# Attention and GELU MLP on one core: seven block products in place of eight in half of the first product of tiles 7 and 8

## The chip, the cores and the metric

The kernel runs on one core of one Trainium2 chip. The core has a matrix engine (TensorE, "PE" in the profile, its weight loads shown as "PEld"), a vector engine (VectorE, "DVE"), a scalar engine (ScalarE, "ACT"), GpSimd ("POOL") and SyncE ("SP"). Each engine takes its own instructions strictly in program order and waits on semaphores for the others; DMA queues move data. Matrix products land in PSUM, eight banks of 128 x 512 f32. The metric is device time in microseconds of one execution. The kernel before took 301.54 us, median of 13 runs from 298.81 to 305.87.

## The reference

A sliding-window attention (8 batches, 8 heads, 576 positions, head size 64, window 32 to each side) gives x, a matrix of 4608 tokens by 512; a two-layer MLP with a tanh-approximated GELU follows:

```python
scores = scale * np.matmul(q, k.transpose(0, 1, 3, 2))
scores = np.where(np.abs(pos[:, None] - pos[None, :]) <= window, scores, -1e9)
attn = softmax(scores); attn_out = np.matmul(attn, v)
x = attn_out.transpose(0, 2, 1, 3).reshape(B * S, H * D)     # 4608 x 512
h = x @ w_in                                                 # 512 -> 2048
g = gelu_tanh(h)
return g @ w_out                                             # 2048 -> 512
```

## The kernel before

The tokens are cut into nine tiles of 512 (t = 0 to 8). Each turn of the loop over t does the first product of tile t (x @ w_in and GELU, into gT), then its second product (g @ w_out), and in between the steps of the second product the attention of batch t+1, which makes the x of later tiles. All data are f16 on the way into PE and f32 in PSUM.

*First product.* `ffn_in(t, n)` computes one column, 128 of the 2048 hidden units for the tile's 512 tokens: four matmuls of 128x512 (L544) accumulate over the 512 model dimensions in one PSUM bank. There are sixteen columns, taken in the order n = 0 to 15, which `column` maps to n // 2 + 8 * (n % 2). `gelu` (L552, on ACT) reads the bank and writes that column of gT. The first three columns are begun at the end of the tile before, three quarters of each. Columns 1 and 2 use the two-bank buffer S0; the others go round the banks D, x1 and x0.

*Sums.* After every fourth column `sums` (L587, on DVE) makes four f16 sums of 128x512 from gT: S1 = A21 + A22, S2 = S1 - A11, S3 = A11 - A21, S4 = A12 - S2, where A11 to A22 are the blocks of g (two halves of the hidden units by two halves of the tokens).

*Second product.* `ffn_out(t, i)`, i = 0 to 111, is already in seven block products in place of eight (Winograd's form of Strassen's method); each is sixteen matmuls of 128x256 (L642). The seven pairs are in a list:

```python
WINO = [("A11", "B11", True), ("S2", "T2", True), ("A12", "B21", False), ("S3", "T3", False),
        ("S1", "T1", True), ("A22", "T4", False), ("S4", "B22", False)]
```

True means that the product starts a new accumulation in its bank; products 0, 2, 4 and 6 use bank x1 and products 1, 3 and 5 bank x0. After each product DVE copies or adds the bank into the f32 buffer y4 (M1 at L653, then L655, L657, L662, L665 or L668, L671, L680), and the next product in that bank may start only after that. So product 2 (A12 x B21) waits for the copy of M1. `store` sends the rows of y4 to DRAM from POOL's queue (L604, L606), in the last tile from SP's and ACT's.

*Order.* The order of every engine's instructions is the order of the program text; no scheduler moves them. Lists (`PLAN`, and for tile 7 `{5: "v-1", 31: "x-1"}`) say before which step i of the second product a piece of attention is placed. "v-1" in tile 7 is the last small group of attention: its matmuls (L462, L472) write banks D and O. Tile 8 has no attention in it. POOL issues the loads of v and the stores; SP issues the loads of q and k, which end with tile 5.

Of the kernel before, what the change touches and what calls it, by code (L numbers as in the profile page):

```python
# [36 lines left out]
def cut(b):  # L37
# [19 lines left out]
PLAN_1 = {12: "s0@0 s1@1 s2", 16: "m0 m1", 36: "m2", 45: "v0@1 v1 s-1@0", 52: "x0", 55: "x1", 62: "m-1",  # L57
          69: "s3@0 v2 v-1@1", 73: "m3", 81: "x2", 85: "x-1", 91: "v3 s4@1", 112: "x3 m4"}
PAIR_1 = {17: slice(0, 4), 40: slice(4, 8)}
# [5 lines left out]
RING = 1536  # L65
# [4 lines left out]
def kernel(  # L70
# [264 lines left out]
    def bank(i):  # L335

        return psM.tile([128, 512], FP32, name="mm", tag=f"x{i}")
# [183 lines left out]
    def column(t, n):  # L521

        return n // 2 + 8 * (n % 2) if t else n

    def ffn_in(t, n, d0=0, d1=4, then=True):
        fc = column(t, n)
        if t not in gTs:
            gTs[t] = gp.tile([128, NF, 512], FP16, name="gT", tag="gT")
        if d0 == 0:
            if t == 0:  # L530
                i = n % 8
                if i in (4, 6):
                    phs["S"] = psS.tile([128, 2, 512], FP32, name="ph2", tag=f"S{i // 2 - 2}")
                phs[fc] = psO.tile([128, 512], FP32, name="ph", tag="DO"[i]) if i < 2 else \
                    bank(i - 2) if i < 4 else phs["S"][:, i % 2, :]
            else:
                i = 3 if n in (1, 2) else 0 if n == 0 else (2, 1, 0)[n % 3]
                if n == 1:
                    phs["S"] = psS.tile([128, 2, 512], FP32, name="ph3", tag="S0")
                phs[fc] = bank(i) if i < 2 else phs["S"][:, n - 1, :] if i == 3 else \  # L540
                    psO.tile([128, 512], FP32, name="ph", tag="D")
        ph = phs[fc]
        for dc in range(d0, d1):
            nc.tensor.matmul(ph, w_in16[:, dc, fc * 128:fc * 128 + 128],  # L544
                             xT[:, dc, t * 512 % RING:t * 512 % RING + 512],
                             start=(dc == 0), stop=(dc == 3))
        if d1 == 4 and then:
            gelu(t, n)

    def gelu(t, n):  # L550
        fc = column(t, n)
        nc.scalar.activation(gTs[t][:, fc, :], phs[fc], AF.Gelu_apprx_tanh)  # L552
        if t and n % 4 == 3:
            sums(t, n // 4)

    wino = {}

# [18 lines left out]
        dst, x, y = wino["todo"][i]  # L576
        eng.tensor_tensor(dst, x, y, op=ALU.subtract)

    def sums(t, i):

        g, r = gTs[t], slice(2 * i, 2 * i + 2)
        A11, A21, A12, A22 = (g[:, r0 + 2 * i:r0 + 2 * i + 2, c:c + 256]
                              for r0 in (0, 8) for c in (0, 256))
        S1, S2, S3, S4 = (wino[f"S{n}"][:, r, :] for n in (1, 2, 3, 4))
        for dst, x, y, op in ((S1, A21, A22, ALU.add), (S2, S1, A11, ALU.subtract),
                              (S3, A11, A21, ALU.subtract), (S4, A12, S2, ALU.subtract)):
            nc.vector.tensor_tensor(dst, x, y, op=op)  # L587

    out_v = out.rearrange("(b p j) f -> b j p f", b=B, j=4)
# [226 lines left out]
    for t in range(NT):  # L816
        b = t + 1
        att = b < B
        if t:
            for fc in range(begun):  # L820
                ffn_in(t, fc, 3, 4, then=False)
            for fc in range(begun):
                gelu(t, fc)
            if att and b > 1:
                parts = cast_and_turn(b)
            for fc in range(begun, NF):
                ffn_in(t, fc)
                if t == 1 and fc == 3:
                    parts[0]()
                    combine(4, nc.vector)  # L830
                if t == 1 and 6 <= fc < 10:
                    cast_v(2, fc - 6)
                if t == 1 and 9 <= fc < 14:
                    parts[1](fc - 9)
                if t == 1 and fc == 8:
                    trans_tails(1, psO.tile([128, 8, 128], FP16, name="pt", tag="O"))
                if t == 2 and fc in (8, 9):
                    store(0, *later[1 if fc == 8 else 3])
                if t > 1 and fc == 8 and att:
                    pair_v(b, nc.vector.tensor_copy)  # L840
        plan = PLAN_0 if not t else PLAN_1 if t == 1 else PLAN if att else {5: "v-1", 31: "x-1"} if t == B - 1 else {}

        def group(g):
            return (b, g) if g >= 0 else (b - 1, 4)
# [6 lines left out]
        for i in range(113 if t else 65):  # L851
            if t and i == (4 if t > 1 else 46) and b + 1 < B:
                nc.gpsimd.tensor_copy(after, KLs[b % 2][:, 3, 0:1])
                load_v(b + 1)
            for act in plan.get(i, "").split():
                kind, at = act[0], int(act[act.index("@") + 1:]) if "@" in act else None
                g = int(act[1:].split("@")[0])
                if kind == "w":
                    if g == 3:
                        cast_w(wo[g], w_out16[:, 12:16, :], cs=(0, 1), on_dve=(0,))  # L860
                    else:
                        cast_w(wo[g % 3], w_out16[:, 4 * (g % 3):4 * (g % 3) + 4, :], on_act=(1, 3),
                               cs={1: range(4), 2: (0, 1), 5: (2, 3)}[g])
                elif kind == "e":
                    cast_vt(1) if g == 4 else cast_v(1, g)
                elif kind == "k":
                    cast_early(1, g, (nc.vector, nc.vector))
                    if g == 2:
                        cast_tails(0, nc.gpsimd, even)
                elif kind == "t":  # L870
                    trans_tails(0, spare(at)[0], even)
                elif kind == "r":
                    trans_pair(1, g, *spare(at), copy=nc.scalar.copy if g == 2 else nc.vector.tensor_copy)
                elif kind in "np":
                    pair = psS.tile([128, 2, 512], FP32, name="ps_od", tag=f"S{at}")
                    for x in range(2):
                        if kind == "n":
                            sum_up(1, g + x, pair[:, x, :], groups[(1, g + x)])
                        else:
                            ods[g + x] = (pair[:, x, :], lts[g + x])  # L880
                            times(1, g + x, pair[:, x, :], groups.pop((1, g + x)))
                    if kind == "n":
                        n = size(1, g)
                        lts[g], lts[g + 1] = lt4[:, g, :], lt4[:, g + 1, :]
                        for x in range(2):
                            nc.scalar.activation(lts[g + x][:, 0:n], pair[:, x, 0:n], AF.Ln)
                        for x in range(2):
                            nc.scalar.activation(lts[g + x][:, 0:n], lts[g + x][:, 0:n], AF.Exp, scale=-1.0)
                elif kind == "u":
                    cast_w(wo[g], w_out16[:, 12:16, :], on_act=(3,), cs=(2, 3))  # L890
                    cast_tails(1, nc.gpsimd)
                    load_qk(2)
                elif kind == "c":
                    if g == 1:
                        B12 = combine_w()
                    combine(g, nc.vector)
                elif kind == "s":
                    score(*group(g), at)
                    if t == 1 and g == 4:
                        load_table(gelu_set)  # L900
                elif kind == "d":
                    pair_chunk(b, g, nc.vector.tensor_copy)
                elif kind == "m":
                    mask(*group(g))
                elif kind == "v":
                    bb, gg = group(g)
                    o, d = weigh(bb, gg, at)
                    ods[g] = (o, invert(bb, gg, d))
                    if t and g < 0 and b + 1 < B:
                        load_vt(b + 1)  # L910
                    if t > 1 and g == (3 if att else -1):
                        load_table(gelu_set)
                else:
                    spread(*group(g), *ods[g])
            if t == 1 and i == 30:
                cast_vt(2)
                store(0, *later[0])
                store(0, *later[2])
            if t == 1 and i in PAIR_1:
                pair_v(2, nc.vector.tensor_copy, PAIR_1[i])  # L920
            if t == 0 and i < 64:
                ffn_out_0(*ORDER_0[i])
            elif t and i < 112:
                ffn_out(t, i)
# [36 lines left out]
```

## Time and profile before

| what | us |
|---|---|
| median of 13 runs | 301.54 |
| the profiled execution | 301.52 |
| its span, first to last instruction | 299.8 |
| tile 7: first L544 that completes a column, start | 244.33 |
| tile 7: third block product (product 2), start | 260.47 |
| tile 8: first L544 that completes a column, start | 271.14 |
| tile 8: third block product, start | 286.51 |
| end of the last matmul, about | 295.4 |

The profile is of one execution. A row of the timeline gives the start in us from the span's start, the length, the engine, the line of the kernel, the operation, what it writes and reads with partitions x elements, and in brackets how long the engine had been idle and whose result ended that. The starts of one engine's instructions can lie closer together than their lengths, because they overlap in its pipeline. The granted clock of PE was 1.00 in every stretch that holds matrix work.

### The profile page before, as it was taken

To read this page: it belongs to the slowest core of one execution; us is meant where nothing else is said; L and a number is where in the kernel's file an instruction comes from. 1 tells how busy PE (TensorE), PEld (TensorE's weight loads), DVE (VectorE), ACT (ScalarE), POOL (GpSimd) and SP (SyncE) were. 2 spreads that over 40 slices of the span, in tenths; PEclk is the share of its full clock that TensorE was granted. 3 is DMA by queue.
4 is the path that set the end of the run, shared out by engine and by line. 5 is a ranking of instruction groups with operands and counts; after the bars stand their busy time and mean duration, and the time that the engine had idled before them with its cause. 6 is when DMAs were issued, how large, how long until landed. Compare 5 with 4: busy or idle time off the path is not lost.

```text
span 299.8 us, 7125 instructions
## 1 busy us (share of the span) xinstructions
PE 286.8 (96%) x2893; PEld 179.6 (60%) x2893; DVE 195.0 (65%) x439; ACT 193.7 (65%) x307; POOL 90.7 (30%) x141
## 2 busy tenths in 40 slices
PE   7889899899999899999999999999999999999994
PEld 2534434446774488447854885478547864784583
DVE  4752577897976866957687769766876635442452
ACT  4866666679676776578567956695678666706600
POOL 3435415302654050605070606060700050015000
PEclk9999999999999999999999999999999999999999
DMA  7999998999899999898998996989792031004013
GB/s 221 266 300 384 357 277 231 246 202 204 213 207 192 239 238 159 143 121 210 180 204 145 225 168 148 148 201 178 113 186 33 3 100 43 2 3 137 2 35 105
DMA packets 116518, 50.73 MB, mean 169 GB/s; under 512 B 98007, under 2 KB 110039, under 8 KB 116486
## 3 DMA queue, kind: packets, MB, share of 16 engines
q1 hardware_dynamic: 87428, 37.88, 61.9%
q0 software_dynamic: 27936, 11.35, 25.5%
q10 hardware_dynamic: 1122, 1.06, 1.1%
q8 instruction: 22, 0.36, 0.5%
q14 instruction: 10, 0.08, 0.1%
HBM read 36.70 MB, written 9.44 MB: 154 GB/s over the span
## 4 chain that ended last, share of the span: by engine, by line
PE 64%; DMA 22%; SPq 7%; ACT 3%; DVE 1%; issue 1%; POOL 0%; DVEq 0%; ACTq 0%
PE mm L642 28%; PE mm L544 15%; PE ph L544 13%; DMA KT<-k 6%; DMA wst<-in_moe_w_in_dram 5%; DMA kr<-in_k_dram 4%; DMA tr<-in_q_dram 4%; PE ps_s L435 2%; PE ps_d L462 2%; DMA wst<-in_moe_w_out_dram 2%; SPq L173 2%; DMA tr<-in_k_dram 2%; PE ps_o L472 2%; SPq L227 2%; ACT gT L552 1%; SPq L149 1%
## 5 line engine op out<-in xcount | busy, mean ns | idle before, releaser
L544 PEld LDWEIGHTS <-w_in 128*128 128x128 f16 x576 | 55.9, 98 | 66.2 <-DVE w_in L215 0.6
L544 PE MATMUL mm<-xT,w_in 128*128 128x512 f16 x304 | 74.7, 379 | 0.0
L552 ACT ACTIVATE gT<-mm 128x512 f16<-128x512 f32 x76 | 45.1, 597 | 40.1 <-PE mm L544 39.4
L544 PE MATMUL ph<-xT,w_in 128*128 128x512 f16 x272 | 68.2, 379 | 0.3 <-POOL w_in L758 0.3
L606 POOL DMA_DIRECT2D out_dram<-y x55 | 32.2, 594 | 89.7 <-DVE y L671 75.6
L642 PEld LDWEIGHTS <-s 128*128 128x128 f16 x512 | 49.6, 98 | 6.0
L587 DVE TENSOR_TENSOR s<-gT 128x512 f16<-128x512 f16 x64 | 27.2, 425 | 33.2 <-ACT gT L552 33.2
L552 ACT ACTIVATE gT<-ph 128x512 f16<-128x512 f32 x68 | 37.9, 599 | 13.0 <-PE ph L544 13.0
L642 PE MATMUL mm<-t,s 128*128 128x256 f16 x376 | 44.7, 273 | 0.0
L642 PEld LDWEIGHTS <-gT 128*128 128x128 f16 x384 | 36.0, 98 | 6.6
L448 ACT ACTIVATE pe<-ps_s 128x960 f16<-128x960 f32 (+1 forms) x31 | 29.5, 975 | 14.2 <-PE ps_s L435 14.1
L642 PE MATMUL mm<-w_out,gT 128*128 128x256 f16 x256 | 32.8, 273 | 0.0
L95 ACT ACT_TABLE_LOAD x18 | 23.1, 1283 | 2.2 <-issue 1.9
L498 ACT ACTIVATE lt<-lt 128x480 f32<-128x480 f32 (+3 forms) x36 | 21.1, 585 | 1.1
L497 ACT ACTIVATE lt<-ps_d 128x480 f32<-128x480 f32 (+2 forms) x28 | 15.6, 555 | 9.3 <-PE ps_d L462 6.2
L457 DVE TENSOR_TENSOR pe<-pe,band 128x960 f16<-128x960 f16 x28 | 18.3, 668 | 1.2 <-ACT pe L448 1.2
L181 POOL DMA_DIRECT2D V<-in_v_dram x20 | 17.9, 913 | 1.1 <-issue 1.0
L472 PEld LDWEIGHTS <-V 128*64 128x64 f16 x520 | 14.0, 111 | 6.0 <-DVE V L191 1.4
L642 PE MATMUL mm<-t,gT 128*128 128x256 f16 x128 | 16.3, 273 | 0.0
L435 PE MATMUL ps_s<-QT,KT 64*64 64x128 f16 (+3 forms) x576 | 13.5, 216 | 2.3 <-DMA KT<-k 1.6
L435 PEld LDWEIGHTS <-KT 64*64 64x64 f16 x576 | 10.0, 106 | 8.4 <-issue 3.6
L642 PE MATMUL mm<-w_out,s 128*128 128x256 f16 x120 | 14.4, 273 | 0.0
(112 smaller groups left out, 324.3 us busy)
## 6 DMA issues: line engine op xcount, KB each, us to landing
kr<-in_k_dram SPq DMA_DIRECT2D x31, 256.0 KB, 11.5
qr<-in_q_dram SPq DMA_DIRECT2D x6, 1024.0 KB, 8.4
wst<-in_moe_w_in_dram SPq DMA_DIRECT2D x7, 512.0 KB, 8.4
V<-in_v_dram POOLq DMA_DIRECT2D x20, 128.0 KB, 8.8
wst<-in_moe_w_out_dram SPq DMA_DIRECT2D x2, 1024.0 KB, 12.0
wst<-in_moe_w_out_dram SPq DMA_DIRECT2D x4, 512.0 KB
qr<-in_q_dram SPq DMA_DIRECT2D x7, 256.0 KB, 6.8
out_dram<-y POOLq DMA_DIRECT2D x6, 192.0 KB, 5.7
```

The source lines that it names most:

```text
L95: nc.scalar.add_instruction(mybir.InstLoadActFuncSet(name=nc.get_next_instruction_name(), act_func_set_id=which, ins=[], outs=[]))
L181: nc.gpsimd.dma_start(V[:, c, :, :], v[b, :, 128 * c:128 * c + 128, :].rearrange("h p d -> p h d"))
L435: nc.tensor.matmul(sides[h][64 * half:64 * half + 64, 4 * n * r:4 * n * r + 4 * n].rearrange("k (j p) -> k j p", j=4)[:, :, p0 - q0:p1 - q ...
L448: nc.scalar.activation(pe, ps[:, :, 0:w], AF.Exp, scale=SCALE)
L457: nc.vector.tensor_tensor(pe, pe, m.rearrange("k (o j) p -> k o j p", o=1).broadcast_to(list(pe.shape)), op=ALU.mult)
L472: nc.tensor.matmul(o[64 * h:64 * h + 64, cols].rearrange("d (j p) -> d j p", j=4)[:, :, p0 - q0:p1 - q0], Vs[b % 2][:, slot, 2 * pr + h, : ...
L498: nc.scalar.activation(lt[:, 0:n], lt[:, 0:n], AF.Exp, scale=-1.0)
L544: nc.tensor.matmul(ph, w_in16[:, dc, fc * 128:fc * 128 + 128], xT[:, dc, t * 512 % RING:t * 512 % RING + 512], start=(dc == 0), stop=(dc = ...
L552: nc.scalar.activation(gTs[t][:, fc, :], phs[fc], AF.Gelu_apprx_tanh)
L587: nc.vector.tensor_tensor(dst, x, y, op=op)
L606: eng.dma_start(out_v[b, j, q0 + p:q0 + p + e, cols], yo[m:m + e, cols])
L642: nc.tensor.matmul(pys["apart"][:, 0:256] if apart else py[:, blk, :], lhsT, wino[w][:, f, :], start=(new and i % (8 if one else 16) == 0) ...
```

## The change

In tiles 7 and 8 the sixteen columns of the first product are split. Columns 0 to 3 and 12 to 15 stay as they were. The other eight are two units, A and B; each is a product of 2 x 2 blocks (two halves of 512 hidden units, from rows 2j and 8 + 2j of gT, by two halves of the 512 tokens, summed over two halves of the model dimensions) and is now made of the same seven block products as the second product, four matmuls of 128x256 each.

The sums of weights are made once: of unit B by POOL in tiles 3 and 4, of unit A by DVE and POOL in tile 6 (`in_w`). The differences of x are made by DVE, four ops of 128x512 f16, before tile 7's columns and in tile 7's second product for tile 8 (`in_x`). In a tile the products of each unit use three banks: "a" (products 0, 1, 3 and 5, bank O for A, x1 for B), "b" (product 2, a half of S1) and "c" (products 4 and 6, a half of S0). Three copies per unit take the running sum out of bank "a" into f32 buffers `sa` and `sb` (DVE, ACT, DVE), three additions on DVE put banks "b" and "c" onto them, and GELU reads three of the four blocks from these buffers and the fourth from bank "a". The order of all this is written out in the list MIX: a digit is a column, A0 a product, s0A a copy, cA00 an addition, g a GELU, t the first two and u the last two of the four sums of a group. Columns 3, 12 and 14 use bank D, columns 13 and 15 bank x0.

```diff
+MIX = ("3 g3 A0 s0A B0 s0B A2 B2 cA00 cB00 A1 s1A A4 B1 s1B gA00 gB00 B4 t0 u0 12 A3 s3A B3 s3B g12 cA11 cB11 13 "
+       "A5 B5 gA11 gB11 g13 14 gA10 gB10 A6 B6 cA01 cB01 g14 15 gA01 gB01 t1 t2 g15 t3 u1 u2 u3").split()
+UNITS = {"A": 1, "B": 2}
...
-                i = 3 if n in (1, 2) else 0 if n == 0 else (2, 1, 0)[n % 3]
+                i = 3 if n in (1, 2) else 0 if n == 0 else (2, 1, 0)[n % 3] if t < NT - 2 else (2, 0)[n % 2 if n > 3 else 0]
...
+    def in_w(eng, unit, *which):
...
+        for x in which:
+            dst, a, b, op = ((S1, A21, A22, ALU.add), (S2, S1, A11, ALU.subtract),
+                             (S3, A11, A21, ALU.subtract), (S4, A12, S2, ALU.subtract))[x - 1]
+            eng.tensor_tensor(dst, a, b, op=op)
+    def in_x(t):
...
+        xc = hp.tile([128, 4, 2, 256], FP16, name="xc", tag="q16" if t % 2 else "k16")
...
+        for dst, a, b in ((T1, B12, B11), (T2, B22, T1), (T3, B22, B12), (T4, B21, T2)):
+            nc.vector.tensor_tensor(dst, a, b, op=ALU.subtract)
+    def in_product(unit, n):
+        a, w, new = WINO[n]
+        if n == 0:
+            phs[unit, "a"] = psO.tile([128, 512], FP32, name="pu", tag="O") if unit == "A" else bank(1)
+        elif n in (2, 4):
+            which = "b" if n == 2 else "c"
+            if unit == "A":
+                phs[which] = psS.tile([128, 2, 512], FP32, name="pu2", tag="S1" if n == 2 else "S0")
+            phs[unit, which] = phs[which][:, "AB".index(unit), :]
+        ps = phs[unit, "b" if n == 2 else "c" if n in (4, 6) else "a"]
+        lhs, rhs = mixed[unit, "w"][a], mixed["x"][w]
+        for h in range(2):
+            for d in range(2):
+                nc.tensor.matmul(ps[:, 256 * h:256 * h + 256], lhs[:, d, 128 * h:128 * h + 128], rhs[:, d, :],
+                                 start=(n in (0, 2, 4) and h == d == 0), stop=(h == d == 1), skip_group_check=True)
+    def in_mixed(t):
+        if "A" not in mixed:
+            mixed["A"] = rawp.tile([128, 3, 512], FP32, name="sa", tag="qr")
+            mixed["B"] = rawp.tile([128, 3, 512], FP32, name="sb", tag="kr")
+        place = {"00": (0, "b"), "01": (1, "c"), "11": (2, "c")}
+        for step in MIX:
+            kind, rest = step[0], step[1:]
+            if kind in UNITS:
+                in_product(kind, int(rest))
+            elif kind == "s":
+                n, unit = int(rest[0]), rest[1]
+                (nc.scalar.copy if n == 1 else nc.vector.tensor_copy)(
+                    mixed[unit][:, (0, 1, None, 2)[n], :], phs[unit, "a"])
+            elif kind == "c":
+                x, which = place[rest[1:]]
+                x = mixed[rest[0]][:, x, :]
+                nc.vector.tensor_tensor(x, phs[rest[0], which], x, op=ALU.add)
+            elif kind == "g" and rest[0] in UNITS:
+                r, c, j = int(rest[1]), int(rest[2]), UNITS[rest[0]]
+                src = phs[rest[0], "a"] if rest[1:] == "10" else mixed[rest[0]][:, place[rest[1:]][0], :]
+                nc.scalar.activation(gTs[t][:, 8 * r + 2 * j:8 * r + 2 * j + 2, 256 * c:256 * c + 256],
+                                     src.rearrange("p (h c) -> p h c", h=2), AF.Gelu_apprx_tanh)
+            elif kind == "g":
+                fc = column(t, int(rest))
+                nc.scalar.activation(gTs[t][:, fc, :], phs[fc], AF.Gelu_apprx_tanh)
+            elif kind in "tu":
+                sums(t, int(rest), slice(0, 2) if kind == "t" else slice(2, 4))
+            else:
+                ffn_in(t, int(step), then=False)
...
-    def sums(t, i):
+    def sums(t, i, which=slice(0, 4)):
...
-                              (S3, A11, A21, ALU.subtract), (S4, A12, S2, ALU.subtract)):
+                              (S3, A11, A21, ALU.subtract), (S4, A12, S2, ALU.subtract))[which]:
...
-            for fc in range(begun, NF):
+            if t >= NT - 2:
+                if t == NT - 2:
+                    in_x(t)
+                in_mixed(t)
+            for fc in range(begun, NF if t < NT - 2 else 0):
...
+            if t == NT - 2 and i == 60:
+                in_x(t + 1)
+            if t in (3, 4) and i == 92:
+                in_w(nc.gpsimd, "B", *((1, 2) if t == 3 else (3, 4)))
+            if t == NT - 3 and i in (86, 90):
+                in_w(*((nc.vector, "A", 1, 2) if i == 86 else (nc.gpsimd, "A", 3, 4)))
```

More of the change, by code (lines that the diff above doesn't have):

```diff
@@ L554, in gelu @@
             sums(t, n // 4)
+    mixed = {}
+    def in_w(eng, unit, *which):
+        i = UNITS[unit]
+        A11, A12, A21, A22 = (w_in16[:, d:d + 2, c + 256 * i:c + 256 * i + 256] for c in (0, 1024) for d in (0, 2))
+        if (unit, "s") not in mixed:
+            halves = [(rawp if unit == "A" else yp).tile([128, 2, 2, 256], FP16, name="wc" + unit + str(x),
+                                                         tag=("qr", "kr")[x] if unit == "A" else "yo") for x in range(2)]
+            mixed[unit, "s"] = [half[:, x] for half in halves for x in range(2)]
+        S1, S2, S3, S4 = mixed[unit, "s"]
+        mixed[unit, "w"] = dict(A11=A11, A12=A12, A22=A22, S1=S1, S2=S2, S3=S3, S4=S4)
+        for x in which:
+            dst, a, b, op = ((S1, A21, A22, ALU.add), (S2, S1, A11, ALU.subtract),
+                             (S3, A11, A21, ALU.subtract), (S4, A12, S2, ALU.subtract))[x - 1]
+            eng.tensor_tensor(dst, a, b, op=op)
@@ new lines, in in_x @@
+    def in_x(t):
+        pos = t * 512 % RING
+        B11, B12, B21, B22 = (xT[:, d:d + 2, pos + c:pos + c + 256] for d in (0, 2) for c in (0, 256))
+        xc = hp.tile([128, 4, 2, 256], FP16, name="xc", tag="q16" if t % 2 else "k16")
+        T1, T2, T3, T4 = (xc[:, x] for x in range(4))
+        mixed["x"] = dict(B11=B11, B21=B21, B22=B22, T1=T1, T2=T2, T3=T3, T4=T4)
+        for dst, a, b in ((T1, B12, B11), (T2, B22, T1), (T3, B22, B12), (T4, B21, T2)):
+            nc.vector.tensor_tensor(dst, a, b, op=ALU.subtract)
```

## The prediction

> **What bounds the kernel now.** I read the page's busy shares first, then the chain that ended last, then the granted clock, and last the timeline of the two tiles that the change touches. The page's first and fourth parts:
>
> ```profile
> PE 286.8 (96%) x2893; PEld 179.6 (60%) x2893; DVE 195.0 (65%) x439; ACT 193.7 (65%) x307; POOL 90.7 (30%) x141
> ...
> PE 64%; DMA 22%; SPq 7%; ACT 3%; DVE 1%; issue 1%; POOL 0%; DVEq 0%; ACTq 0%
> ```
>
> TensorE (PE) is busy nearly always and carries most of the chain; DVE is a third idle on average. That average is no help: what counts is which engine is last inside tiles 7 and 8. Busy time by stretch (columns: length, then busy us and instructions of PE, PEld, DVE, ACT, POOL, then clock, DMA share, GB/s); the rows are tile 7's first product and second, tile 8's first and second, and the end:
>
> ```profile
> 242.28:255.99 13.71, 13.71 (x67) 6.25 (x64) 5.32 (x14) 8.67 (x16) 3.99 (x8) 1.00 0.27 77
> 255.99:269.09 13.10, 12.96 (x123) 11.35 (x122) 6.13 (x11) 4.33 (x6) 0.45 (x1) 1.00 0.00 1
> 269.09:282.80 13.71, 13.71 (x67) 6.25 (x64) 5.32 (x14) 8.49 (x15) 5.00 (x10) 1.00 0.27 78
> 282.80:296.30 13.50, 12.60 (x114) 10.96 (x112) 6.58 (x13) 0.74 (x2) 0.00 (x0) 1.00 0.17 52
> 296.30:299.80 3.50, 0.00 (x0) 0.00 (x0) 0.00 (x0) 0.00 (x0) 0.00 (x0) 0.80 0.39 99
> ```
>
> Both first products are gapless on PE, at full clock. Now the hand-over from first to second product of tile 8 (start, length, what; in brackets the idle time before):
>
> ```profile
> 282.15 1.03 PE L544 MATMUL ph<-xT,w_in 128*128 128x512 f16 x4
> ...
> 283.01 1.91 PE L642 MATMUL mm<-w_out,gT 128*128 128x256 f16 x16
> 283.21 0.60 ACT L552 ACTIVATE gT<-ph 128x512 f16<-128x512 f32 x1 [0.27 <-PE ph L544]
> 283.84 0.42 DVE L587 TENSOR_TENSOR s<-gT 128x512 f16<-128x512 f16 x1 [1.90 <-ACT gT L552]
> 284.30 0.42 DVE L587 TENSOR_TENSOR s<-s,gT 128x512 f16<-128x512 f16 x1
> 284.64 0.42 DVE L587 TENSOR_TENSOR s<-gT 128x512 f16<-128x512 f16 x1
> ...
> 284.76 1.91 PE L642 MATMUL mm<-t,s 128*128 128x256 f16 x16
> 284.98 0.42 DVE L587 TENSOR_TENSOR s<-gT,s 128x512 f16<-128x512 f16 x1
> 285.31 0.68 DVE L653 COPY y<-mm 128x512 f32<-128x512 f32 x1
> ...
> 286.51 1.91 PE L642 MATMUL mm<-w_out,gT 128*128 128x256 f16 x16
> ```
>
> After the last GELU only four sums stand on DVE ahead of the copy of M1 (L653). The third block product (286.51) accumulates into the bank that this copy reads, so it may not start before it; the copy ends at 285.99, 0.52 us early. That slack is the number to watch. Tile 7 shows one stall, in the chain: the D bank is not free for the group "v-1" until column 15's GELU is done.
>
> ```profile
> 255.50 0.88 PE ph L544 x4
> 256.40 0.61 ACT gT L552
> 257.05 0.35 PE ps_d L462 x2
> ```
>
> **The change, part by part.** All times below are us after a tile's first L544 matmul that completes a column (tile 8: 271.14; tile 7: 244.33).
>
> *Removed on PE.* Per tile, 32 matmuls of 512 become 56 of 256. Eight of 512 take 1.73 (chain), so 0.2157 each; sixteen of 256 take 286.51 - 284.76 = 1.75, so 0.109 each, their weight loads included. 32 x 0.2157 = 6.90 against 56 x 0.109 = 6.12: 0.78 saved per tile if nothing waits. The first product would end at 11.1 in place of 11.86.
>
> *Removed in tile 7.* Bank D is last used by column 14, not 15, so its stall (256.75 to 257.05) goes: 0.30. Next is the GELU of column 14, which I place at 11.64, before PE gets there (11.8).
>
> *Added on DVE per tile.* Four copies and six additions from PSUM, 128x512 f32. Rows L653 and L662 have 0.69; the next op may start 0.61 after (258.92 to 259.53 in tile 7). Bounds on the spacing 0.61 and 0.69; I take 0.61, which is measured. The sums keep their count of sixteen: 0.46 after an op whose result is needed (283.84 to 284.30), otherwise 0.34.
>
> *Added and moved on ACT.* Two copies (bounds 0.59 as L622's and 0.63 as L498's 512; 0.59 taken) and six of the sixteen GELUs now read f32 from SBUF. No row has such a GELU; a GELU from PSUM is spaced 0.49 (272.05 to the end of three, 1.57 later), and an exponential of 512 from SBUF (L498) lasts 0.63. Bounds 0.49 and 0.60, taken 0.52: the 0.03 by which L498's row exceeds L552's 0.60.
>
> *The new schedule*, in program order per engine, with PE results visible 0.42 (512) and 0.31 (256) after the last matmul's start as in the rows above, and 0.06 for a release of PE. PE: column 3 to 1.51, A0 1.95, B0 2.38, A2 2.82, B2 3.26, A1 3.69, A4 4.13, B1 4.57, B4 5.00, column 12 5.87, A3 6.30, B3 6.74, column 13 7.60, A5 8.04, B5 8.48, column 14 9.34, A6 9.78, B6 10.21, column 15 11.10. DVE: s0A 2.18, s0B 2.79, cA00 3.49 (it waits for B2 too), cB00 4.10, t0 and u0 4.71 to 6.27, then s3A not before A3 is visible: 6.53, s3B 7.14, cA11 7.75, cB11 8.36 to 9.05. So no bank makes PE wait, within 0.1, until here. ACT: gA11 8.44, gB11 9.05 (it waits for cB11), g13 9.57, gA10 10.06, gB10 10.55, g14 11.04, gA01 11.53 to 12.16, gB01 to 12.68, g15 12.57 to 13.17. In the kernel before, the last GELU ended at 283.81 - 271.14 = 12.67; so ACT is later though PE is earlier.
>
> *The added wait.* DVE's t1 (S1, S2 of unit A) waits for gA01, the ACT instruction before it, and all other sums but group 0's stand behind it: t1, t2, t3, u1, u2, u3, twelve ops. From 12.19: three pairs of 0.46 + 0.34 and six of 0.34 are 4.44, so the M1 copy starts at 16.63 and ends at 17.32. Behind DVE stands PE: block product n=0 starts at 11.21 (x1 is held by gB10), n=1 at 13.23 (x0 is held by g15), its rows 4 and 6 wait for t2 and t3 (0.36 and 0.58), and n=2 waits for M1 until 17.38, 1.46 of it idle. Before, n=2 started at 286.51 - 271.14 = 15.37: tile 8 loses 2.01. In tile 7 it started at 260.47 - 244.33 = 16.14; the group v-1 (0.46 on PE) now hides inside the wait, so n=2 again starts at 17.38: 1.24 lost. The 0.78 and the 0.30 are inside these differences. From n=2 on each eviction keeps its place, about 1 us of idle DVE before each, so nothing is won back.
>
> *The rest, at nothing, with its cover.* in_x of tile 7: four ops of 0.34 to 0.46 on DVE after 243.35, done at about 0.6, and s0A is at 2.18. in_x of tile 8, about 1.5, between C11 and U3 in tile 7: DVE has 1.05 free there and n=5 needs U3 only 1.75 after n=3; 0.5 late is covered, and without that cover it would cost 0.5. Two unit-A sums in tile 6 (0.8): DVE is idle 0.70 before 240.84; the copy after it may slip 0.1, and bank x0 is wanted only at 242.39. The six sums on POOL in tiles 3, 4 and 6 go ahead of the stores in its queue, which waits there for L671 (23.95 before 241.83); POOL casts of 512 last 0.6 to 0.87, so two delay stores by about 2 at most, if they run late, and nobody reads the stores but the next tile's evictions, a tile later. No DMA is added, SP's queue is untouched. The Trainium skill (SBUF — State Buffer, "Who interferes with whom") says that a DVE op with two SBUF inputs and a GpSimd op that reads SBUF lock each other out; no row here shows a GpSimd sum beside DVE. By that page each of the six could hold DVE up by one op, an estimate of 1 each, which the idle DVE of those spots would take.
>
> *Sum.* +2.01 + 1.24 = +3.25. The profiled execution took 301.52 (span 299.80 and 1.72 around it), next to the median of 301.54: 301.52 + 3.25 = **304.8**. With the unknowns at their cheap ends (spacing of PSUM reads 0.55, below any row, and no release time) n=2 starts at 17.0, which is +2.5; with all at their dear ends (ACT 0.60, DVE 0.70) at 17.86, which is +4.2. So 304.0 to 305.7.
>
> **Rivals.**
>
> *Faster (the other side): DVE's twelve sums are done when PE wants M1.* Then tile 8 reaches n=2 at 11.10 + 3.49 = 14.59 (-0.78), tile 7 at 15.05 (-1.09): 299.65. For it: DVE's share in tile 8's second product is only 6.58 of 13.50. Against it: 0.34 and 0.46 are measured, and the order on DVE is fixed. It decides when M1 is copied 1.63 earlier in each tile, that is when the 5.1 from gA01 to M1's end become 3.5.
>
> *About level: ACT reaches gA01 sooner.* cA01 ends at 11.13, and ACT gets there only at 11.53 with five GELUs queued since 9.05. If it kept up, t1 could start at 11.2, 1.0 earlier per tile: +1.2, 302.7. Against it: gB11 cannot precede cB11, which hangs on A3.
>
> *Slower still: PE's clock falls in the new gaps.* PE gets waits of 0.1, 0.3, 0.4, 0.6 and 1.5 in a row of 6 us. The clock row falls below 1.00 only in the last 3.5, where PE does nothing: 0.80. A loss of 0.2 over 3.5 is 0.7 per tile: +1.4, 306.2. The Trainium skill (TensorE: Matmul & The Clock Gate, "What's actually happening") puts the gate at an idle window of about 3.4, and no gap here is that long, so by it nothing is added; the same page ("A second HAM failure mode: psum-queue depth-cycling") warns that frequent short idling between bank groups makes the clock swing. By that the price would be half the work of one window, an estimate of 1.7 per tile and 308.2 in all; no row here shows it.
>
> *It does not do what it says:* the 256-column blocks run at the weight loads' pace. L642's rows exclude it: same shape, 0.109.
>
> **How the numbers follow.** Forecast 0.70, level 0.13 (0.09 of it within 0.5%, the rest just above), clock 0.08, faster 0.08, the rest 0.01. A measurement of this kernel tells about 0.5% (1.5 us) from no change; so faster 0.08, same 0.09, slower 0.83. The range takes in the forecast's 304.0 to 305.7, the level case and the clock's 306.2, and half a us of scatter of medians (single runs go from 298.81 to 305.87): 302.3 to 306.7. It leaves out the faster case.
>
> **What would show it.** Right: in tile 8 the first product ends about 0.75 sooner; the M1 copy is preceded on DVE by twelve sums without a gap; the third block product's wait, 1 to 2 us, is put down to that copy; n=2 begins near 17.4 in both tiles. Wrong: sums starting before gA01, an idle DVE before M1, or PE waiting inside the first product (then the PSUM reads are dearer than 0.61). A granted clock under 1.00 between 255 and 300 would be the clock rival.

## The result and the profile after

The changed kernel takes **307.39 us** (median of 11 runs, 304.55 to 313.40) against 301.94 for the kernel before (median of 48). The ratio is 1.018, with a 95% interval from 1.0142 to 1.0218: it is slower by 5.4 us (4.3 to 6.6). The forecast was 304.8, with 302.3 to 306.7 as its range: the direction was right, the size was outside. Ratios here and below are made from undisturbed executions of both kernels, so a ratio can differ from the quotient of two medians.

Line numbers of the kernel after: L553 matmuls of the columns, L605 the new block products, L625 additions, L561, L629 and L633 GELU, L670 sums of gT, L725 second product, L736 copy of M1, L738 and L740 the next evictions, L466 masks of attention, L471 the matmuls of attention's denominators, L580 sums of weights, L190 and L194 loads of v. From here on, "after" a tile's start means after its first L553 that completes a column (L544 in the kernel before); these starts are 247.14 and 275.17 for tiles 7 and 8.

First part of the page, busy time of each engine:

```profile
PE 287.3 (94%) x2941; PEld 183.9 (60%) x2941; DVE 215.0 (70%) x469; ACT 194.3 (64%) x311; POOL 97.0 (32%) x147
```

PE's busy time is nearly the same (286.8 before), while the span grew from 299.8 to 305.7. So the loss is waiting. Busy time by stretch (length, then PE, PEld, DVE, ACT, POOL, clock, DMA share, GB/s), here from each tile's start on: tile 7's first product and second, tile 8's first product and, to 302.20, its second:

```profile
247.14:258.05 10.91, 10.91 (x80) 7.63 (x79) 7.46 (x15) 7.19 (x14) 2.21 (x5) 1.00 0.30 89
258.05:275.17 17.12, 15.38 (x134) 12.01 (x132) 11.69 (x27) 5.86 (x9) 2.50 (x5) 1.00 0.06 16
275.17:286.40 11.23, 11.23 (x81) 7.72 (x80) 7.30 (x14) 7.51 (x15) 2.92 (x6) 1.00 0.26 72
286.40:302.20 15.80, 13.05 (x113) 10.69 (x111) 9.92 (x22) 1.96 (x4) 0.00 (x0) 1.00 0.16 46
```

Both first products are still without a gap, and the first matmul of the second product starts at 11.23 in both tiles (258.37 and 286.40). In the second products PE is idle for 1.74 and 2.75 (the latter about 0.8 of it behind the last matmul). The hand-over of tile 8, from the timeline:

```profile
286.70 0.65 ACT L629 ACTIVATE gT<-sa 128x512 f16<-128x512 f32 x1
287.22 0.65 ACT L629 ACTIVATE gT<-sb 128x512 f16<-128x512 f32 x1
287.38 0.43 DVE L670 TENSOR_TENSOR s<-gT 128x512 f16<-128x512 f16 x1 [0.51 <-ACT gT L629]
...
289.92 1.26 PE L725 MATMUL mm<-t,s 128*128 128x256 f16 x10 [0.40 <-DVE s L670]
...
291.45 0.42 DVE L670 TENSOR_TENSOR s<-gT,s 128x512 f16<-128x512 f16 x1
291.79 0.68 DVE L736 COPY y<-mm 128x512 f32<-128x512 f32 x1
292.53 1.69 PE L725 MATMUL mm<-w_out,gT 128*128 128x256 f16 x14 [1.34 <-DVE y L736]
```

GELU gA01 starts at 286.70 - 275.17 = 11.53, twelve sums follow on DVE without a gap, the copy of M1 starts at 16.62, and the third block product at 17.36. Tile 7 shows the same:

```profile
263.76 0.68 DVE L736 COPY y<-mm 128x512 f32<-128x512 f32 x1
...
264.50 1.69 PE L725 MATMUL mm<-w_out,gT 128*128 128x256 f16 x14 [1.34 <-DVE y L736]
```

The chain that ended last has the same two links in tile 8, three of the twelve sums and the copy:

```profile
290.87 1.01 DVE s L670 x3
291.87 0.61 DVE y L736
292.48 0.04 issue
292.53 4.53 PE mm L725 x40
```

The third block product starts, after the tile's start:

| | tile 7 | tile 8 |
|---|---|---|
| before | 16.14 | 15.37 |
| forecast for after | 17.38 | 17.38 |
| after | 17.36 | 17.36 |
| lost, forecast / measured | 1.24 / 1.22 | 2.01 / 1.99 |

This part accounts for 3.2 us, as forecast. Most of the rest came from a place where the forecast had put nothing. The stretch from tile 4's start to tile 5's, before and then after:

```profile
153.02:183.50 30.48, 30.48 (x331) 20.02 (x330) 22.64 (x55) 21.54 (x33) 10.65 (x17) 1.00 1.09 177
```

```profile
153.96:186.31 32.35, 30.86 (x332) 20.09 (x330) 24.40 (x55) 21.66 (x33) 13.88 (x19) 1.00 1.03 163
```

It grew by 1.87. DVE has the same 55 operations there and is busy 1.76 longer, so it is not that it does more: the same operations take longer. POOL has two more, the sums of weights. The timeline of the kernel before at the masks of attention:

```profile
166.29 3.59 POOL L181 DMA_DIRECT2D V<-in_v_dram  x4
168.55 1.22 DVE L457 TENSOR_TENSOR pe<-pe,band 128x960 f16<-128x960 f16 x2
170.49 0.37 PE L462 MATMUL ps_d<-pe,ones 128*64 128x480 f16 x2
```

and of the kernel after:

```profile
166.97 3.59 POOL L190 DMA_DIRECT2D V<-in_v_dram  x4 [0.34 <-issue]
169.49 3.46 DVE L466 TENSOR_TENSOR pe<-pe,band 128x960 f16<-128x960 f16 x2
170.52 0.72 POOL L194 DMA_DIRECT2D V<-in_v_dram  x1
171.23 1.20 POOL L580 TENSOR_TENSOR wcB<-w_in 128x512 f16<-128x512 f16 x1
172.35 1.61 POOL L580 TENSOR_TENSOR wcB<-w_in,wcB 128x512 f16<-128x512 f16 x1
173.01 0.39 PE L471 MATMUL ps_d<-pe,ones 128*64 128x480 f16 x2 [1.42 <-DVE pe L466]
```

Two masks take 3.46 in place of 1.22, and PE waits 1.42 for the second of them. The sums stand at step 92 in the program text, but POOL has nothing between its loads of v and step 92, so it runs them right behind the loads, at 17.3 after the tile's start, in the thick of attention.

The profiled execution's other differences are 0.11 before tile 1, +1.16 in tile 1, -0.04 in tile 2, -0.29 in tile 3 and about 0 in tiles 5 and 6; the 1.16 goes with a wait of PE for copies of v (1.21 in that profile, nothing to speak of in the kernel before, 0.26 to 1.00 in the profiles of the runs below), at a place that nothing in the change touches. With 1.87 in tile 4, 1.22 in tile 7 and 1.87 from tile 8's start to the end of the span, that gives the 5.9 between the two spans.

### The profile page after: what moved, and what is told of

The parts are those of the page before. It is cut to its first block, busy times and chain, and to the rows that moved or that the text cites. A ratio compares the mean times of both kernels' runs of the same rounds, so it can differ in the third digit from the quotient of the medians.

```text
span 305.7 us, 7275 instructions
## 1 busy us (share of the span) xinstructions
PE 287.3 (94%) x2941; PEld 183.9 (60%) x2941; DVE 215.0 (70%) x469; ACT 194.3 (64%) x311; POOL 97.0 (32%) x147
## 5 line engine op out<-in xcount | busy, mean ns | idle before, releaser
L553 PEld LDWEIGHTS <-w_in 128*128 128x128 f16 x512 | 49.7, 98 | 58.4 <-ACT w_in L850 1.7
L553 PE MATMUL ph<-xT,w_in 128*128 128x512 f16 x256 | 64.1, 379 | 1.5 <-ACT w_in L850 1.2
L553 PE MATMUL mm<-xT,w_in 128*128 128x512 f16 x256 | 63.7, 379 | 0.0
L561 ACT ACTIVATE gT<-mm 128x512 f16<-128x512 f32 x60 | 35.6, 597 | 36.9 <-PE mm L553 36.3
L725 PEld LDWEIGHTS <-s 128*128 128x128 f16 x512 | 49.3, 98 | 8.0 <-DVE s L670 1.8
L725 PE MATMUL mm<-t,s 128*128 128x256 f16 x376 | 45.2, 273 | 1.0 <-DVE s L670 0.8
L725 PEld LDWEIGHTS <-gT 128*128 128x128 f16 x384 | 36.0, 98 | 9.9 <-issue 3.5
L561 ACT ACTIVATE gT<-ph 128x512 f16<-128x512 f32 x58 | 32.2, 599 | 10.5 <-PE ph L553 10.5
L670 DVE TENSOR_TENSOR s<-gT 128x512 f16<-128x512 f16 x64 | 27.1, 424 | 12.0 <-ACT gT L561 11.0
L725 PE MATMUL mm<-w_out,gT 128*128 128x256 f16 x256 | 32.8, 273 | 2.7 <-DVE y L736 2.7
L466 DVE TENSOR_TENSOR pe<-pe,band 128x960 f16<-128x960 f16 x28 | 21.5, 783 | 0.9 <-ACT pe L457 0.9
L190 POOL DMA_DIRECT2D V<-in_v_dram x20 | 17.9, 906 | 1.3 <-PE ps_s L444 0.6
L725 PE MATMUL mm<-t,gT 128*128 128x256 f16 x128 | 16.3, 273 | 0.0
L670 DVE TENSOR_TENSOR s<-s,gT 128x512 f16<-128x512 f16 x32 | 14.9, 465 | 1.1
```

Source lines behind the costliest of these rows:

```text
L190: nc.gpsimd.dma_start(V[:, c, :, :], v[b, :, 128 * c:128 * c + 128, :].rearrange("h p d -> p h d"))
L466: nc.vector.tensor_tensor(pe, pe, m.rearrange("k (o j) p -> k o j p", o=1).broadcast_to(list(pe.shape)), op=ALU.mult)
L725: nc.tensor.matmul(pys["apart"][:, 0:256] if apart else py[:, blk, :], lhsT, wino[w][:, f, :], start=(new and i % (8 if one else 16) == 0) ...
```

## The experiments

**Theory.** Two separate losses: (a) the twelve sums ahead of M1's copy in tiles 7 and 8, 3.2 us; (b) POOL's sums of weights, which hold up DVE in tile 4, about 1.9 us. **Rivals:** for (a), that the new block products, copies or additions cost time of themselves, or that a later wait takes the copy's place; for (b), that the longer tile 4 is scatter, comes from the loads of v, or comes from any use of SBUF by POOL.

**The sums of unit B on DVE instead of POOL.** At the same step 92:

```diff
-                in_w(nc.gpsimd, "B", *((1, 2) if t == 3 else (3, 4)))
+                in_w(nc.vector, "B", *((1, 2) if t == 3 else (3, 4)))
```

> Edit: the four weight sums of unit B move from POOL to DVE, at the same step 92 of tiles 3 and 4. Theory: in the changed kernel they run on POOL right after the loads of v in its queue (171.23 to 173.96 in tile 4), hold two masks of DVE (3.46 in place of 1.22), and PE then waits 1.42 and 0.36; that is 1.87 of the loss. With the sums on DVE at step 92, where DVE is idle about 1 us between evictions, tile 4 is back at about 30.5 from first completed column to the next tile's, and the total is 3.2 to 3.5 above before (in place of 5.4). Rival (the extra 2 us beyond tiles 7 and 8 are scatter in when DMAs land at the start): the total stays 5 to 5.5 above before.

Measured: ratio to the kernel before 1.0099 (1.0063 to 1.0134), +3.0 us (1.9 to 4.0). Tile 4 takes 30.48 again, the third block product stays at 17.36 and 17.37. What is left is (a).

**The sums of weights alone.** The sums stay on POOL in tiles 3, 4 and 6, nobody reads them; tiles 7 and 8 are as before.

```diff
...
-            if t >= NT - 2:
-                if t == NT - 2:
-                    in_x(t)
-                in_mixed(t)
-            for fc in range(begun, NF if t < NT - 2 else 0):
+            for fc in range(begun, NF):
...
-            if t == NT - 2 and i == 60:
-                in_x(t + 1)
```

> Edit: only the six weight sums and two on DVE are kept (their results are not used); the columns of tiles 7 and 8 and their sums are as before. Theory: tile 4 takes 32.3 in place of 30.5, tiles 7 and 8 are as before, the total is 1.9 above before (range 1.3 to 2.5). Rival (the sums are free, as predicted): within 0.5 of before.

Measured: 1.0083 (1.0040 to 1.0127), +2.5 us (1.2 to 3.8). The stall is in its profile too:

```profile
171.73 3.65 DVE L466 TENSOR_TENSOR pe<-pe,band 128x960 f16<-128x960 f16 x2
...
175.43 0.39 PE L471 MATMUL ps_d<-pe,ones 128*64 128x480 f16 x2 [1.60 <-ACT lt L507]
```

The wait is put down to an ACT operation here, which ended at 175.39, with the masks at 175.38; the two cannot be told apart, but it is the masks that are longer than before. The profile is of an execution of 308.26 us, in which the granted clock was 0.75 from 174 to 178, so its length of tile 4, 34.13, says little about the 32.3 that were expected. (a) alone and (b) alone, 3.0 and 2.5, add to 5.5, beside the measured 5.4; with intervals of 1 us and more to each side this fits two separate losses, but does not prove that they add exactly.

**The same sums on POOL, behind the stores.** They are issued after the tile's last step, so POOL runs them in the next tile's first product, where DVE has no masks.

```diff
-            if t in (3, 4) and i == 92:
-                in_w(nc.gpsimd, "B", *((1, 2) if t == 3 else (3, 4)))
...
+        if t in (3, 4):
+            in_w(nc.gpsimd, "B", *((1, 2) if t == 3 else (3, 4)))
```

> Edit: the sums of unit B stay on POOL but stand behind the stores of tiles 3 and 4 in its queue, so that they run in the first products of tiles 4 and 5. Theory (what counts is which DVE work they meet): they hold DVE's sums s there by 1 to 2.3, and PE does not need these before the second product, so tile 4's loss goes and the total is 3.2 to 3.6 above before. Rival (POOL's use of SBUF costs the same wherever it stands): the loss moves to tile 5 and the total stays 5 or more above before.

Measured: the six runs scattered from 302.49 to 310.84 and gave no interval. It was run again:

> The same kernel as in the run with POOL's sums behind the stores, taken again for an interval. In that run's profile tiles 4 and 5 took 30.48 and 30.41, as before. Theory: 3.2 to 3.6 above before. Rival (the loss moves to tile 5): 5 or more above before.

Measured: 1.0120 (1.0079 to 1.0161), +3.6 us (2.4 to 4.9); tile 4 takes 30.49. So POOL may do the sums, if it does them elsewhere. There too DVE was held, but PE did not wait for it: a sum took 1.26 in place of 0.42. Beside POOL's first sum the last of four casts took 1.88 (three of them are in the row below, 2.68; in the kernel before four take 1.58), although a cast has a single input, in SBUF:

```profile
154.78 2.68 DVE L367 CAST qt<-qt 16x512 f16<-16x512 f32 x3
...
156.00 1.17 POOL L580 TENSOR_TENSOR wcB<-w_in 128x512 f16<-128x512 f16 x1
...
157.25 1.90 POOL L580 TENSOR_TENSOR wcB<-wcB,w_in 128x512 f16<-128x512 f16 x1
...
158.16 1.26 DVE L670 TENSOR_TENSOR s<-s,gT 128x512 f16<-128x512 f16 x1
```

**Memsets in place of the sums.** Same place on POOL, two memsets of 128x1024 in tiles 3 and 4 instead of unit B's sums; otherwise as in the run of the weights alone.

```diff
-                in_w(nc.gpsimd, "B", *((1, 2) if t == 3 else (3, 4)))
...
+                for half in mixed["B", "z"]:
+                    nc.gpsimd.memset(half, 0.0)
```

> Edit: as the run with the weight sums alone, but in tiles 3 and 4 POOL fills the two buffers with zeros (128x1024 each) in place of the sums, so that it writes about as long and reads nothing; tiles 7 and 8 are as before. Theory (a DVE op that reads two SBUF operands and a POOL op that reads SBUF shut each other out): the masks keep their 1.22 for two, tile 4 takes 30.5, the total is within 0.6 of before. Rival (any POOL access to SBUF holds the mask, or POOL's place in the queue delays something else): the mask is stretched by 1 or more and the total is 1.5 or more above before.

Measured: 1.0005 (0.9951 to 1.0059), +0.2 us (-1.5 to 1.8). The profile can't say why, though: there tile 4 began at 151.23, and POOL reached the memsets at 170.95, 19.7 after that, when both masks were done. POOL's loads of v wait for a transfer of k that is done at nearly the same time in these three profiles (165.74 before, 166.44 after, 166.16 here), while the tile's start shifts by 2.7 us (153.02, 153.96, 151.23). So whether POOL's work and the masks meet can differ from one execution to the next. The next three runs put POOL's work ahead of the loads of v in tile 4, where it meets DVE in any case.

**Memsets, sums and copies on POOL, ahead of the loads of v.** Tiles 7 and 8 are as in the kernel before, unit B's sums are left out, and unit A's in tile 6 stay; in tile 4:

```diff
                 nc.gpsimd.tensor_copy(after, KLs[b % 2][:, 3, 0:1])
+                if t == 4:
...
+                    for half in halves + halves:
+                        nc.gpsimd.memset(half, 0.0)
                 load_v(b + 1)
```

> The kernel before, with four memsets of 128x1024 f16 (0.95 each in the run with memsets behind the loads of v, so 3.8 in a row) on POOL in tile 4, ahead of the loads of v instead of behind them. POOL reached that place at 12.5 to 15.1 after the tile's first column in the runs so far, the two masks run at 15.5 to 16.8 where nothing holds them, so one or the other memset runs beside them. Theory: what holds DVE is a POOL operation that reads SBUF; a memset only writes. Then the two masks take 1.22, PE has no wait there, and tile 4's stage is 30.4 to 30.5. Rival: any POOL operation on SBUF holds DVE. Then the masks start or end with a memset and take 2 or more, and tile 4's stage is 31.3 or more. The loads of v start 3.8 later, which both theories price at nothing in tile 4.

> The same place, four sums of 128x512 f16 on POOL (two inputs in SBUF, 1.15 to 1.6 each, so 4.6 to 6.4 in a row) in place of the four memsets; their results are read by nothing. Theory, that POOL reading SBUF holds DVE's operations with two inputs: the two masks take 2.2 to 3.5 instead of 1.22, and tile 4's stage is 31.3 to 32.6 where the profile catches the masks beside the sums. Rival, that the stall in tile 4 came from the loads of v beside the masks and not from the sums: masks 1.22 (the loads now start after them), stage 30.4 to 30.5.

> The same place, two copies of 128x1024 f16 from SBUF to SBUF on POOL (one input) in place of the four memsets. Theory, that any read of SBUF by POOL holds DVE: the masks are stretched, to 2 or more, and tile 4's stage is 31.0 or more. Rival, that only a POOL operation with two inputs holds it: masks 1.22 and stage 30.4 to 30.5.

Measured in one execution each (the third has four copies, not the two its expectation names). The whole times, 301.13, 308.59 and 302.83 with the kernel before at 300.20, say little: in the second, PE waits 4.58 for a transfer of k in tile 2, where the edit has not begun. So only tile 4 is read. With memsets:

```profile
165.25 3.63 POOL L940 MEMSET wcB<- 128x1024 f16 x4
...
165.81 0.42 DVE L670 TENSOR_TENSOR s<-s,gT 128x512 f16<-128x512 f16 x1
...
168.19 1.22 DVE L466 TENSOR_TENSOR pe<-pe,band 128x960 f16<-128x960 f16 x2
```

With sums:

```profile
171.00 5.23 POOL L941 TENSOR_TENSOR wcB<-w_in 128x512 f16<-128x512 f16 x4
...
171.36 1.26 DVE L670 TENSOR_TENSOR s<-s,gT 128x512 f16<-128x512 f16 x1
172.54 1.37 DVE L670 TENSOR_TENSOR s<-gT 128x512 f16<-128x512 f16 x1
173.84 1.37 DVE L670 TENSOR_TENSOR s<-gT,s 128x512 f16<-128x512 f16 x1
175.14 0.68 DVE L736 COPY y<-mm 128x512 f32<-128x512 f32 x1
```

With copies:

```profile
165.79 4.56 POOL L940 COPY wcB<-w_in 128x1024 f16<-128x1024 f16 x4
...
165.84 1.26 DVE L670 TENSOR_TENSOR s<-s,gT 128x512 f16<-128x512 f16 x1
167.03 1.25 DVE L670 TENSOR_TENSOR s<-gT 128x512 f16<-128x512 f16 x1
168.21 1.25 DVE L670 TENSOR_TENSOR s<-gT,s 128x512 f16<-128x512 f16 x1
```

Beside memsets DVE's sums and masks run at full speed and tile 4 takes 30.48. Beside POOL's sums and copies DVE gets one operation done per POOL operation: its starts are 1.18, 1.30 and 1.30 apart beside sums of 5.23 / 4 = 1.31, and 1.19 and 1.18 apart beside copies of 4.56 / 4 = 1.14. Tile 4 takes 32.46 and 32.10. So one input read on POOL is enough to hold these operations, and a write alone, of these memsets, is not. The rival of the loads of v falls as well: with sums, DVE is held before the loads start at 176.17. Here the masks meet only the tail of POOL's work (1.57 and 1.45 in place of 1.22), and PE waits mostly for M1's copy (1.03 and 0.79), which stands behind the held sums.

**M1's copy ahead of half the sums.** S3 and S4 of the three late groups are made later, behind the copy:

```diff
-       "A5 B5 gA11 gB11 g13 14 gA10 gB10 A6 B6 cA01 cB01 g14 15 gA01 gB01 t1 t2 g15 t3 u1 u2 u3").split()
+       "A5 B5 gA11 gB11 g13 14 gA10 gB10 A6 B6 cA01 cB01 g14 15 gA01 gB01 t1 t2 g15 t3").split()
...
+            if t >= NT - 2 and i in (16, 32):
+                for x in range(1, 4):
+                    sums(t, x, slice(2, 3) if i == 16 else slice(3, 4))
```

> Edit: of the twelve sums at the end of the first product the six of S3 and S4 go behind the copy of M1, S3 before step 16 and S4 before step 32 of the second product. Theory: M1's copy then starts right after t3, at 14.6 after the tile's first completed column in place of 16.6, and the third block product starts at 15.9 in place of 17.36 in both tiles: 2.9 less than the changed kernel, so 2.5 above before. Rival (the sums have to be done anyway, so DVE stays last): the wait moves to the fourth or a later block product, and the total stays within 0.7 of the changed kernel, 4.7 or more above before.

Measured: 1.0035 (0.9989 to 1.0081), +1.1 us (-0.3 to 2.4). By the stretches it is what was expected: the third block product starts at 15.86 in both tiles, 1.50 sooner than after, and tile 4 still takes 32.63. (The profile is of an execution of 308.61 us; the granted clock was 1.00 in the stretches read here.) The total is 1.4 under the 2.5 that was expected, just outside the interval; why is not shown. The rival, a wait that moves on to the fourth product, is refuted; the fourth product's sums come from 294.54 on, in time, and no bracket stands behind the product:

```profile
292.33 0.68 DVE L736 COPY y<-mm 128x512 f32<-128x512 f32 x1
292.93 1.08 DVE L670 TENSOR_TENSOR s<-gT 128x512 f16<-128x512 f16 x3
293.57 1.91 PE L725 MATMUL mm<-w_out,gT 128*128 128x256 f16 x16
...
294.54 1.09 DVE L670 TENSOR_TENSOR s<-gT,s 128x512 f16<-128x512 f16 x3
295.32 1.91 PE L725 MATMUL mm<-t,s 128*128 128x256 f16 x16
```

**The reverse: six more sums in the kernel before.** S3 and S4 of the three late groups are simply made a second time ahead of M1's copy in tiles 7 and 8, with no new block products:

```diff
+        if t >= NT - 2 and n == 15:
+            for x in range(1, 4):
+                sums(t, x, slice(2, 4))
...
```

> Edit: the kernel before, in which tiles 7 and 8 make the S3 and S4 of the last three groups a second time, six more sums of 0.34 on DVE ahead of M1's copy; no block products in the first product. Theory: M1's copy starts 2.04 later than DVE could before; the third block product goes from 286.51 to 288.1 in tile 8 (0.5 of slack is used up first) and from 260.47 to 261.3 in tile 7; the total is 2.4 above before. Rival (the copy of M1 does not decide when PE goes on): within 0.5 of before.

Measured: 1.0134 (1.0057 to 1.0212), +4.1 us (1.7 to 6.4), against 2.4 expected. The interval is wide, and the profiled execution also waits 3.57 for a transfer of k in tile 2, which the edit does not touch (1.35 in the kernel before). Tiles 7 and 8 are sharp: the third block product starts at 16.93 and 16.92, that is 0.79 and 1.55 later than before, and the wait is put down to the copy, as in the changed kernel:

```profile
290.07 0.42 DVE L590 TENSOR_TENSOR s<-gT,s 128x512 f16<-128x512 f16 x1
290.41 0.69 DVE L656 COPY y<-mm 128x512 f32<-128x512 f32 x1
291.14 1.91 PE L645 MATMUL mm<-w_out,gT 128*128 128x256 f16 x16 [1.40 <-DVE y L656]
```

So a queue of sums ahead of this copy is enough; the new block products are not needed for the loss.

**All repairs together.** Unit B's sums on DVE and half the late sums behind M1's copy, as in the two edits above, and a tail of MIX that lets g13 ahead of gA11 on ACT:

```diff
-       "A5 B5 gA11 gB11 g13 14 gA10 gB10 A6 B6 cA01 cB01 g14 15 gA01 gB01 t1 t2 g15 t3 u1 u2 u3").split()
+       "A5 B5 g13 gA11 gB11 14 gA10 gB10 A6 B6 cA01 cB01 g14 15 gA01 gB01 t1 t2 g15 t3").split()
...
```

> Edit: the changed kernel with unit B's weight sums on DVE, the sums of S3 and S4 behind M1's copy, and column 13's GELU ahead of the second block's GELUs of A and B, so that GELU A01 starts when cA01 is done. All seven block products stay. Theory (two causes, the twelve sums before M1 and POOL's sums in tile 4): the third block product starts at about 15.5 after the tile's first completed column, which is 0.6 sooner than before in tile 7 and 0.15 later in tile 8; tile 4 takes 30.5; the total is within 0.5% of before (-0.5 us). Rival (the seven products with their copies and additions cost time in themselves): 1.5 us or more above before.

Measured: 300.56 us, ratio 0.9961 (0.9924 to 0.9997), -1.2 us (-2.3 to -0.1): the seven block products in place of eight are kept, and this version is faster than after and, by an interval that only just leaves out zero, slightly faster than before. The third block product starts at 15.44 in both tiles, 0.70 sooner than before in tile 7 and 0.07 later in tile 8:

```profile
283.81 0.68 DVE L737 COPY y<-mm 128x512 f32<-128x512 f32 x1
...
285.05 1.91 PE L726 MATMUL mm<-w_out,gT 128*128 128x256 f16 x16
```

The rival, that the new products, copies and additions cost 1.5 or more of themselves, is refuted.

## Why the prediction was right in direction and wrong in size

*Removed on PE (0.78 per tile):* right. The second product begins at 11.23, against 11.21 in the forecast, and PE has no wait to speak of before it.

*The costs of copies, additions and GELUs:* right. Additions start 0.61 apart (285.58 to 286.19), as was taken. A GELU from SBUF lasts 0.65 and the next starts 0.52 after (286.70 to 287.22); 0.52 was the estimate. gA01 starts at 11.53, as forecast.

*The added wait (+1.24 and +2.01):* right, to 0.02 each. The runs show it from both sides: half of the twelve sums taken out of DVE's queue ahead of M1's copy gave back 1.50 in each tile; six put in took 0.79 and 1.55.

*The rest, at nothing, with its cover:* **this step failed.** The prediction said: "The six sums on POOL in tiles 3, 4 and 6 go ahead of the stores in its queue", and that a hold-up of DVE, "an estimate of 1 each", is one "which the idle DVE of those spots would take". The size of the hold-up was about right (in tile 4 the two masks took 2.24 longer beside two sums); its cover was not there. The sums were placed by what stands behind them in POOL's queue, the stores, and not by what stands ahead of them, nothing but the loads of v. The rule that each engine goes through its own list at its own pace was applied to DVE in tiles 7 and 8 and not to POOL in tile 4. And "those spots" were not read there: at the masks of tile 4 DVE has little to give, as PE takes their result 0.7 after they end (170.49 against 169.77 before).

A price could have been read, too. It is true that no row before shows a GpSimd sum beside DVE, but casts on POOL stand beside masks and sums on DVE, as here in the profile of the kernel before:

```profile
38.43 0.87 POOL L215 CAST w_out<-wst 128x512 f16<-128x512 f32 x1 [2.25 <-DMA wst<-in_moe_w_out_dram]
...
38.74 1.07 DVE L457 TENSOR_TENSOR pe<-pe,band 128x960 f16<-128x960 f16 x1
```

This mask took 1.07 where an undisturbed one takes 0.65; a sum at 73.12 took 0.83 in place of 0.42 beside a cast at 72.88.

The Trainium skill (SBUF — State Buffer, "Who interferes with whom") had named the mechanism: an exclusive lock between a DVE operation with two SBUF inputs and a GpSimd operation that reads SBUF. The runs agree with it for sums and masks (1.18 to 1.30 per held DVE operation, none beside memsets, and the copy of M1, whose only input is in PSUM, not held, 0.68); the held cast shows that here two inputs in SBUF were not needed. Price: 1.87 in tile 4 of the profile after, +2.5 (1.2 to 3.8) over the runs of the sums alone. In tile 3 the same sums stretch a mask to 1.61 and in tile 6 a sum to 1.71, and there PE does not wait; the cover that the prediction counted on existed in two places of three.

With this term the forecast would have been 3.25 + 1.87 = 5.1, beside the measured 5.4 (4.3 to 6.6).

*The rivals.* Faster: refuted; in tile 8 M1's copy starts at 16.62 after the tile's start, 2.45 later than before (285.31 - 271.14 = 14.17). ACT sooner: refuted, gA01 where forecast. PE's clock: 1.00 in all four stretches of tiles 7 and 8, so no part of the loss in this profile is the clock's. Weight loads as the pace: no; the blocks of the new first products leave no gap.

## What to carry to other kernels

The place of an instruction is where its engine's own queue comes to it, so before an extra operation is priced at nothing on a side engine, look up what that engine has queued ahead of it, and what the neighbours do at that moment. GpSimd operations that read SBUF are not free beside DVE operations that read it too: here POOL's sums and copies and DVE's sums and masks took turns, mostly one for one, so such work belongs where nobody waits for DVE. And on an engine that works in order, count what stands ahead of the copy that frees a PSUM bank: six sums moved behind it were worth 1.5 us per tile, here more than the matmuls saved.

## What was not expected of the hardware

DVE was held somewhat before POOL's sums start in the record: in the profile after, the first of the two masks began at 169.49 and ended at 170.74, about 0.6 late, and the first sum is recorded from 171.23. The hold goes with the sums all the same: in the profiles of the weights alone and of half the sums behind the copy that mask also ends 0.49 ahead of the first sum's start (173.15 and 173.65, 174.79 and 175.28), though it began at other distances from it (1.74, 1.92 and 2.02). Either the recorded start on POOL is late, or the issue of the last load of v (170.52) plays a part beside the sums; alone it does not hold DVE (in the kernel before, masks at 110.02 and 201.63 take 0.66 beside that load, recorded from 110.10 and 201.27). This stays open.

In the profile of the weights alone, PE's granted clock was 0.75 from 174 to 178 and 0.65 in the 2 us after, where 15 block matmuls took 3.25 in place of 1.81; the wait of 1.60 had ended at 175.43. After the wait of 1.42 in the changed kernel, and after one of 1.59 at the same place in the run with half the sums behind the copy, the clock stayed at 1.00. A wait of this length thus need not bring the clock down; whether it did in the one profile, and what else it takes, was not tried.
